# Reordering the first loads of a one-core kernel: w_in blocks paired with x tiles, the first block in column halves, the gate row from GpSimd, x tile 4 ahead of w_z1

## The chip, the core and the metric

The kernel runs on one core of one Trainium2 chip. Times are device microseconds of that core; a profiled execution also has a span, which runs from its first to its last instruction and is about 1.7 us shorter than the device time. The kernel before took 208.58 us (median of 3 runs, 208.38 to 208.61). The runs below were made on several chips, and each is compared with runs of the kernel before on its own chip.

## The reference, cut to what matters

```python
def _B_ref(x, w_in, w_sp, b_sp, w_out):
    z = _gelu(jnp.einsum('bsd,df->bsf', x, w_in))     # x 2048 x 512, w_in 512 x 1376
    z1 = z[..., :Fh].copy()                           # Fh = 688
    z2 = _layernorm(z[..., Fh:], axis=-1)
    g = jnp.einsum('ts,bsf->btf', w_sp, z2) + b_sp[None, :, None]
    return jnp.einsum('bsf,fd->bsd', z1 * g, w_out)
g = _sigmoid((x * gate_w).sum(-1, keepdims=True))
a = _A_ref(x, A_wqkv, A_w_phi, A_wo)                  # linear attention, not touched here
return g * a + (1 - g) * _B_ref(...)
```

The kernel starts with z2, the second half of the product of x and w_in. It contracts over 512, so it needs four blocks of 128 rows of w_in (blocks 0 to 3). The gate's logit rides along: the gate row is placed as column 689 beside the second half of each block.

## The kernel before: the parts that matter

The kernel works on 16 tiles of 128 rows of x. x tiles 0 to 3 are loaded plainly and transposed on TensorE; later tiles come through transposing loads. "Half 0" and "half 1" of a block are its columns 0 to 343 and 344 to 687; half 1 also has the gate's column, so its products need the gate row.

```python
    def load_z2w(eng, dt):                      # one block: 128 rows of 688 bf16, 172 KB
        eng.dma_start(out=w_z2[:, dt, 0:FH], in_=w_in_v[:, dt, FH:F])

    nc.sync.dma_start(out=xs[:, 0, :], in_=x2[0:P, :])
    load_z2w(nc.scalar, 0)
    nc.sync.dma_start(out=xs[:, 1, :], in_=x2[P:2 * P, :])
    load_z2w(nc.scalar, 1)
    load_z2w(nc.sync, 2)
    nc.scalar.dma_start(out=gaterow[0:NDT, :], in_=gate_w.rearrange("(dt p) -> dt p", p=P))
    load_z2w(nc.scalar, 3)
    nc.sync.dma_start(out=xs[:, 2:4, :], in_=...)            # x tiles 2 and 3, 256 KB
    for h in range(2):
        nc.sync.dma_start(out=w_z1[:, 2 * h:2 * h + 2, :], in_=...)
    for i in range(4, 8):
        nc.sync.dma_start_transpose(out=xT[:, :, i * P:(i + 1) * P], in_=...)
    ...
    # z2_first_two: one(tt, dt, j) is the product of x tile tt with half j of block dt
        warm_up(6)                  # 512-column products on constants
        warm_up(5, P)               # 128-column ones
        x_T(0, 0, 1, ...)           # TensorE transposes of x tile 0
        x_T(0, 1, NDT, ..., on_act=True)
        warm_up(3, P)
        one(0, 0, 0)
        x_T(1, 0, 2, ...)
        x_T(1, 2, NDT, ..., on_act=True)
        one(0, 1, 0)
        warm_up(2, P)
        one(1, 0, 0)
        one(1, 1, 0)
        gate_T()                    # gate row -> gate column of w_z2
        one(0, 2, 0)
        one(1, 2, 0)
        for dt in range(2):
            one(0, dt, 1)
            one(1, dt, 1)
        one(0, 2, 1)
        one(1, 2, 1)
        x_T(2, 0, NDT, ...)
        one(0, 3, 0); one(0, 3, 1); z2_out(0, zps[0])
        one(1, 3, 0); one(1, 3, 1); z2_out(1, zps[1])
        x_T(3, 0, NDT, ...)
    # then tiles 2, 3, ... in a steady stream of products
```

The softmax here doesn't subtract the row's maximum and nothing guards it: scores larger than these inputs give would overflow.

## Time and profile before

| kernel before, profiled run | us | view |
|---|---|---|
| span | 206.5 | page |
| TensorE busy | 201.1 (97%) | busy table |
| first transposes of x tile 0 | 3.70 | timeline |
| block 2 of w_in landed | 6.23 | chain of waits |
| last startup transposes end, steady stream begins | 8.63 | chain of waits |

The busy table of the kernel before (us, share of the span, instructions; PE is TensorE, DVE VectorE, ACT ScalarE, POOL GpSimd):

```profile
PE 201.1 (97%) x1530; PEld 120.3 (58%) x1548; DVE 129.1 (63%) x277; ACT 77.0 (37%) x124; POOL 44.6 (22%) x72
```

The waits of TensorE over the whole run. Columns: who waited, for whom, us in total, times, longest:

```profile
PE zp L215 <- PEq L582: 0.8, 1, 0.8
PE zp L184 <- DMA w_z<-in_B_w_in_dram: 0.7, 1, 0.7
```

The first 10 us of the chain of waits. Columns: start, duration, what; "x" counts merged instructions:

```profile
...
1.73 4.50 DMA w_z<-in_B_w_in_dram
...
6.27 1.33 PE zp L184 x8
7.60 0.22 PE pq L273 x4
7.83 0.58 PE zp L184 x4
8.41 0.22 PE pq L273 x4
8.63 1.46 PE zp L184 x10
```

TensorE is full except at the start, where it waits once, for block 2 (issued 1.73, landed 6.23). After it come 12 products (L184) and 8 transposes (L273), then the steady stream at 8.63. I call 8.63 the end of the startup in what follows; the prediction used 8.47, the start in the timeline of the first matmul after the transposes, whose modelled spans overlap. The change can act only on this startup.

### The profile page before, as it was taken

The page shows a single profiled execution, that of the slowest core. Times are in us where ns is not written, and L with a number is a line of the kernel's source. Part 1 is how long each engine was busy: PE and PEld are TensorE (multiplying, and loading weights), DVE is VectorE, ACT ScalarE, POOL GpSimd, SP SyncE. Part 2 cuts the span into 40 slices and gives each one's busy share as a digit, 9 for nine tenths or more (in the row PEclk, how much of TensorE's full clock was granted, in tenths as well). Part 3 has the DMA queues.
Part 4 walks back from the last instruction along what each step waited for, and adds up shares of the span by engine and source line. Part 5 has one row for each costly group of instructions (what it writes and reads, how often), then busy time and mean ns, then how long its engine had stood idle before and what let it go on. Part 6 is the DMA issues. An engine that isn't in the chain of part 4 may idle for free.

```text
span 206.5 us, 3955 instructions
## 1 busy us (share of the span) xinstructions
PE 201.1 (97%) x1530; PEld 120.3 (58%) x1548; DVE 129.1 (63%) x277; ACT 77.0 (37%) x124; POOL 44.6 (22%) x72
## 2 busy tenths in 40 slices
PE   8899999999999999999999999999999999999994
PEld 4666666655566555556565666555455555665543
DVE  3477665656977778879797788555466553633330
ACT  3666677786322243333424032222251126001322
POOL 3020202020532326244242422222204220200000
PEclk9999999999999999999999999999999999999999
DMA  6999399999996026961413218765565667453442
GB/s 184 274 149 210 79 263 211 251 206 259 193 290 136 3 38 127 309 100 22 91 29 63 51 38 116 141 117 68 106 158 39 130 104 190 53 104 75 120 97 81
DMA packets 89147, 27.22 MB, mean 132 GB/s; under 512 B 83144, under 2 KB 89128, under 8 KB 89128
## 3 DMA queue, kind: packets, MB, share of 16 engines
q1 hardware_dynamic: 86384, 24.37, 62.4%
q10 hardware_dynamic: 2744, 2.60, 3.8%
q8 instruction: 12, 0.20, 0.4%
q14 instruction: 7, 0.06, 0.1%
HBM read 4.41 MB, written 2.10 MB: 32 GB/s over the span
## 4 chain that ended last, share of the span: by engine, by line
PE 95%; DMA 2%; issue 1%; ACT 1%; SPq 0%; DVE 0%
PE mm L442 36%; PE zp L184 17%; PE mm L347 13%; PE mm L481 8%; PE mm L387 7%; PE mm L479 7%; DMA w_z<-in_B_w_in_dram 2%; PE at L455 2%; PE kvacc L403 2%; PE mm L484 1%; PE zp L300 0%; ACT z1all L253 0%; ACT wq_p L307 0%; PE pq L273 0%; SPq L120 0%
## 5 line engine op out<-in xcount | busy, mean ns | idle before, releaser
L442 PE MATMUL mm<-z2all,wspT 128*128 128x344 bf16 x512 | 79.9, 309 | 0.0
L442 PEld LDWEIGHTS <-wspT 128*128 128x128 bf16 x512 | 49.0, 98 | 25.7 <-issue 0.4
L184 PE MATMUL zp<-w_z,xT 128*128 128x344 bf16 (+1 forms) x256 | 38.8, 309 | 0.7 <-DMA w_z<-in_B_w_in_dram 0.7
L351 ACT ACTIVATE eq<-mm 128x512 bf16<-128x512 f32 x32 | 17.4, 594 | 51.3 <-PE mm L347 25.6
L355 DVE TENSOR_REDUCE zs<-eq 128x64 f32<-128x1024 bf16 x16 | 19.5, 1220 | 20.4 <-ACT eq L351 20.4
L184 PEld LDWEIGHTS <-xT 128*128 128x128 bf16 x256 | 24.6, 98 | 12.8 <-issue 0.7
L447 DVE SCALAR_TENSOR_TENSOR ucat<-mm,bT,z1all 128x344 bf16<-128x344 f32 x32 | 17.4, 544 | 21.9 <-PE mm L442 21.9
L364 POOL TENSOR_TENSOR eq<-eq,ratio 128x512 bf16<-128x512 bf16 x16 | 16.9, 1059 | 49.9 <-DVE ratio L363 41.7
L351 ACT ACTIVATE ek<-mm 128x512 bf16<-128x512 f32 x32 | 17.3, 600 | 27.4 <-PE mm L347 27.4
L495 ACT ACTIVATE ob<-mm,g_inv 128x512 bf16<-128x512 f32 (+1 forms) x16 | 10.9, 681 | 32.8 <-PE mm L484 28.0
L355 DVE TENSOR_REDUCE zs<-ek 128x64 f32<-128x1024 bf16 x16 | 19.3, 1209 | 2.8 <-ACT ek L351 2.8
L481 PE MATMUL mm<-wspT,uT 128*128 128x512 bf16 (+2 forms) x85 | 20.1, 366 | 0.0
L347 PEld LDWEIGHTS <-xT 128*128 128x128 bf16 x128 | 12.2, 98 | 13.2 <-PE mm L484 0.8
L364 POOL TENSOR_TENSOR ek<-ek,ratio 128x512 bf16<-128x512 bf16 x16 | 16.9, 1059 | 2.6 <-DVE ratio L363 1.6
L387 PE MATMUL mm<-wv_sb,xT 128*128 128x512 bf16 x64 | 16.4, 379 | 0.0
L347 PE MATMUL mm<-wq_p,xT 128*128 128x512 bf16 x55 | 16.0, 379 | 0.5
L347 PE MATMUL mm<-wk_p,xT 128*128 128x512 bf16 x61 | 16.1, 379 | 0.3
L479 PE MATMUL mm<-wspT,oT 128*128 128x512 bf16 (+2 forms) x62 | 15.6, 365 | 0.3
L202 DVE BATCH_NORM_STATS2 bn<-z2all 128x6 f32<-128x344 bf16 x32 | 14.9, 501 | 0.0
L199 ACT ACTIVATE z2all<-zp 128x688 bf16<-128x688 f32 x16 | 11.8, 744 | 7.0 <-PE zp L184 7.0
L253 ACT ACTIVATE z1all<-zp 128x688 bf16<-128x688 f32 x16 | 11.9, 744 | 5.1 <-PE zp L184 4.6
L481 PEld LDWEIGHTS <-uT 128*128 128x128 bf16 x85 | 8.1, 98 | 9.2
(71 smaller groups left out, 143.1 us busy)
## 6 DMA issues: line engine op xcount, KB each, us to landing
out_dram<-ob ACTq DMA_DIRECT2D x15, 128.0 KB, 2.0
wspT<-in_B_w_out_dram SPq DMA_DIRECT2D x2, 640.0 KB, 5.2
w_z<-in_B_w_in_dram SPq DMA_DIRECT2D x2, 344.0 KB, 4.7
w_z<-in_B_w_in_dram ACTq DMA_DIRECT2D x3, 172.0 KB, 3.4
wv_sb<-in_A_wqkv_dram SPq DMA_DIRECT2D x2, 256.0 KB, 2.9
wspT<-in_A_wo_dram SPq DMA_DIRECT2D x2, 256.0 KB, 3.9
xs<-in_A_x_dram SPq DMA_DIRECT2D x2, 128.0 KB, 3.0
xs<-in_A_x_dram SPq DMA_DIRECT2D x1, 256.0 KB, 5.1
```

Of the source, the lines that this page charges most:

```text
L184: nc.tensor.matmul(zp[:, j, 0:n], lhsT=xT[:, dt, tt * P:(tt + 1) * P], rhs=wt[:, dt, j * HF:j * HF + n], start=(dt == 0), stop=(dt == NDT ...
L202: nc.vector.bn_stats(out=bn6[:, tt, j, :], in_=z2v[:, j, :])
L253: nc.scalar.activation(out=z1all[:, tt, :].rearrange("p (j n) -> p j n", j=2), in_=zp[:, :, 0:HF], func=AF.Gelu_apprx_tanh,)
L347: nc.tensor.matmul(ps[:, :], lhsT=xT[:, dt, tt * P:(tt + 1) * P], rhs=w[:, dt, :], start=(dt == 0), stop=(dt == NDT - 1))
L351: nc.scalar.activation(out=e[:, :, a, :], in_=ps[:, :].rearrange("p (h f) -> p h f", f=DH), func=AF.Exp, scale=1.0 - 2.0 * a)
L355: nc.vector.tensor_reduce(out=z[:].rearrange("p h a -> p (h a)"), in_=e[:].rearrange("p h a f -> p (h a) f"), axis=AX.X, op=ALU.add,)
L364: nc.gpsimd.tensor_tensor(out=e[:, :, 1, :], in0=e[:, :, 1, :], in1=ratio[:, :, None].to_broadcast([P, H, DH]), op=ALU.mult)
L387: nc.tensor.matmul(v_ps[:, :], lhsT=xT[:, dt, tt * P:(tt + 1) * P], rhs=wv_sb[:, dt, :], start=(dt == 0), stop=(dt == NDT - 1))
L442: nc.tensor.matmul(gp[:, 0:HF], lhsT=wspT[:, st, tt * P:(tt + 1) * P], rhs=z2all[:, st, j * HF:(j + 1) * HF], start=(st == 0), stop=(st == ...
L447: nc.vector.scalar_tensor_tensor(out=ucat[tt % NU][:, c0 + j * HF:c0 + (j + 1) * HF], in0=gp[:, 0:HF], scalar=bT[:, tt:tt + 1], in1=z1all[ ...
L479: nc.tensor.matmul(acc, lhsT=oT[:, g, :], rhs=wo_t[:, g, c0:c1], start=(g == 0), stop=False)
L481: nc.tensor.matmul(acc, lhsT=uT[:, i + ft, :], rhs=w_main[i][:, ft, c0:c1], start=False, stop=False)
```

## The change

The intent: let each block of w_in flow beside an x tile, with a smaller first block, so that TensorE begins earlier and waits less; take the gate row's issue away from the ACT queue; fetch x tile 4 earlier. Fewer warm-up products fit in front of an earlier start. The diff, cut to its core (the new `first` argument of z_one, which lets half 1 start its sum with block 1, is left out):

```diff
+    nc.gpsimd.dma_start(out=gaterow[0:NDT, :], in_=gate_w.rearrange("(dt p) -> dt p", p=P))
     nc.sync.dma_start(out=xs[:, 0, :], in_=x2[0:P, :])
-    load_z2w(nc.scalar, 0)
+    nc.scalar.dma_start(out=w_z2[:, 0, 0:HF], in_=w_in_v[:, 0, FH:FH + HF])
     nc.sync.dma_start(out=xs[:, 1, :], in_=x2[P:2 * P, :])
     load_z2w(nc.scalar, 1)
-    load_z2w(nc.sync, 2)
-    nc.scalar.dma_start(out=gaterow[0:NDT, :], in_=gate_w.rearrange("(dt p) -> dt p", p=P))
-    load_z2w(nc.scalar, 3)
     nc.sync.dma_start(out=xs[:, 2:4, :], in_=...)
+    load_z2w(nc.scalar, 2)
+    nc.sync.dma_start(out=w_z2[:, 0, HF:FH], in_=w_in_v[:, 0, FH + HF:F])
+    load_z2w(nc.scalar, 3)
+    x_dma_T(4)                       # the transposing load of x tile 4
     for h in range(2):               # w_z1
...
-        warm_up(5, P)
+        warm_up(2, P)
-        x_T(0, 1, NDT, ..., on_act=True)
+        x_T(0, 1, NDT, ...)
-        warm_up(2, P)
+        warm_up(1, P)
...
-        for dt in range(2):
+        for dt in range(1, 3):       # half 1 of block 0 moves behind block 3
             one(0, dt, 1)
             one(1, dt, 1)
-        one(0, 2, 1); one(1, 2, 1)
         x_T(2, 0, NDT, ...)
-        one(0, 3, 0); one(0, 3, 1); z2_out(0, zps[0])
-        one(1, 3, 0); one(1, 3, 1); z2_out(1, zps[1])
+        for tt in range(2):
+            one(tt, 3, 0); one(tt, 0, 1); one(tt, 3, 1); z2_out(tt, zps[tt])
```

More of the change, by code (lines that the diff above doesn't have):

```diff
@@ L118, with x_dma_T @@
     nc.sync.dma_start(out=xs[:, 0, :], in_=x2[0:P, :])
-    load_z2w(nc.scalar, 0)
+    nc.scalar.dma_start(out=w_z2[:, 0, 0:HF], in_=w_in_v[:, 0, FH:FH + HF])
     nc.sync.dma_start(out=xs[:, 1, :], in_=x2[P:2 * P, :])
     load_z2w(nc.scalar, 1)
-    load_z2w(nc.sync, 2)
-    nc.scalar.dma_start(out=gaterow[0:NDT, :], in_=gate_w.rearrange("(dt p) -> dt p", p=P))
-    load_z2w(nc.scalar, 3)
     nc.sync.dma_start(
         out=xs[:, 2:4, :], in_=x2[2 * P:4 * P, :].rearrange("(i p) d -> p i d", p=P))
+    load_z2w(nc.scalar, 2)
+    nc.sync.dma_start(out=w_z2[:, 0, HF:FH], in_=w_in_v[:, 0, FH + HF:F])
+    load_z2w(nc.scalar, 3)
+    def x_dma_T(i):
+        nc.sync.dma_start_transpose(out=xT[:, :, i * P:(i + 1) * P], in_=x2[i * P:(i + 1) * P, :])
+    x_dma_T(4)
     for h in range(2):
@@ L129 @@
             out=w_z1[:, 2 * h:2 * h + 2, :], in_=w_in_v[:, 2 * h:2 * h + 2, 0:FH])
-    for i in range(4, 8):
-        nc.sync.dma_start_transpose(out=xT[:, :, i * P:(i + 1) * P], in_=x2[i * P:(i + 1) * P, :])
+    for i in range(5, 8):
+        x_dma_T(i)
     for q in range(2, NCH):
@@ L180, in pq_tile, with z_one @@
         return psF.tile(shape, dtype, name="pq", tag=next_turn("pq", 2))
-    def z_one(zp, tt, wt, w, dt, j):
+    def z_one(zp, tt, wt, w, dt, j, first=0):
         n = HF if j == 0 else w - HF
@@ L186, in z_one @@
             rhs=wt[:, dt, j * HF:j * HF + n],
-            start=(dt == 0), stop=(dt == NDT - 1),
+            start=(dt == first), stop=(dt == NDT - 1),
         )
@@ L219, in one @@
         def one(tt, dt, j):
-            z_one(zps[tt], tt, w_z2, FH + 1, dt, j)
+            z_one(zps[tt], tt, w_z2, FH + 1, dt, j, first=j)
         warm_up(6)
-        warm_up(5, P)
+        warm_up(2, P)
         x_T(0, 0, 1, pq_tile([P, 1, P], BF16)[:, :, :])
-        x_T(0, 1, NDT, pq_tile([P, 3, P], BF16)[:, :, :], on_act=True)
+        x_T(0, 1, NDT, pq_tile([P, 3, P], BF16)[:, :, :])
         warm_up(3, P)
@@ L236, in z2_first_two @@
         one(1, 2, 0)
-        for dt in range(2):
+        for dt in range(1, 3):
             one(0, dt, 1)
             one(1, dt, 1)
-        one(0, 2, 1)
-        one(1, 2, 1)
         x_T(2, 0, NDT, pq_tile([P, NDT, P], BF16)[:, :, :])
-        one(0, 3, 0)
-        one(0, 3, 1)
-        z2_out(0, zps[0])
-        one(1, 3, 0)
-        one(1, 3, 1)
-        z2_out(1, zps[1])
+        for tt in range(2):
+            one(tt, 3, 0)
+            one(tt, 0, 1)
+            one(tt, 3, 1)
+            z2_out(tt, zps[tt])
         x_T(3, 0, NDT, pq_tile([P, NDT, P], BF16)[:, :, :])
```

## The prediction

> **What bounds the kernel.** TensorE: busy 201.1 of 206.5 us (97%, busy table), 95% of the chain of waits. By the waits view it waits twice: 0.84 us before its first instruction and 0.66 us for a block of w_in. After the last startup transposes at 8.25 us (timeline) it lists no wait, so what the start gains or loses should pass to the end unshortened.
>
> **The start before.** Real work: 16 products (0.147 us apart) and 16 transposes (0.055 us apart): 3.2 us. It begins at 3.70 us, when x tile 0 has landed (issue 0.80 + 2.8), and ends at 8.47: about 1.6 us is lost to loads. Landings (DMA issues view): w_in block 0 3.8, x tile 1 4.5, block 1 4.6, block 2 6.2 (issued 1.73 + 4.5), block 3 6.9, x tiles 2-3 7.3. The chain's only DMA piece is block 2, 1.73 to 6.23. After it 12 products and 8 transposes run almost without a gap, 6.27 to 8.47: 12 x 0.147 + 8 x 0.055 = 2.2 us.
>
> The loads are 1.2 MB. From 2 to 8 us the DMA moves 260 to 357 GB/s (windows): bandwidth and order, not issue. The Trainium skill, "DMA: Bandwidth & Descriptors", section "Issuing engines are not separate DMA queues", says all issuers share the same 16 engines; pairing orders the bytes, it adds no rate.
>
> **The change.**
> - Block 0's first half is 86 KB less ahead of the first products: at 300 GB/s at most 0.3 us (estimate); it and x tile 0 land near 3.4. Three 128-column warm-ups go (0.2 us).
> - Block 2 goes third on the ACT queue, beside x tiles 2-3. About 86 KB fewer are ahead of it: landing 5.6 to 5.9. x tiles 2-3, now third on SP, about 6.3.
> - The first tiles' second-half products of block 0 move behind block 3. After block 2 there are still 12 products and 8 transposes, 2.2 us. But the second half of block 0 and block 3 are now the last bytes, landing 6.7 to 7.2; six products and four transposes (1.1 us) come after them. Startup ends 7.9 to 8.3 (before 8.47): gain 0.2 to 0.6.
> - The gate row on GpSimd frees 0.57 us of ACT issue. Same page, "Specifications": about 1 us to first byte on that path against 0.6. Issued near 1.5, landing estimated by 4.5; PE asks near 5.0.
> - x tile 0's three-block copy moves ACT to DVE: about 0.36 us against 0.48: neutral, block 1 arrives later anyway.
> - x tile 4's transposed load goes ahead of w_z1: 1.26 us of SP issue and 128 KB. w_z1 landed 8.2 and 9.1; now about 9 and 9.8, needed at 10.5 and 11.0. Slack shrinks from 2 to about 1 us.
>
> **Prediction.** 208.2 us, range 207.75 to 208.6. Faster by over 2% 0.01, within 2% 0.98, slower 0.01: the whole loss available is 1.6 us, under 1%.
>
> **What would show it.** The wait for block 2 ends before 6.0 (timeline); a wait appears on block 0's second half, block 3 or x tiles 2-3 near 6.7 to 7.1; the last startup transposes start 0.2 to 0.6 earlier; the first z1 product has no DMA wait; everything later shifts by that amount, durations equal.
>
> **What would make it wrong.** The gate row landing after block 2; w_z1 landing after 10.5, which gives the gain back; landings that follow slow DMA engines rather than bytes, so nothing lands earlier; the clock warming later with fewer warm-ups.

## The result and the profile after

The changed kernel took 208.32 us (median of 4 runs, 208.07 to 208.91); the kernel before 208.60 us (208.38 to 208.63) in runs that include those of the first section. The ratio is 0.9993, with a 95% interval of 0.9969 to 1.0017: the same.

The same three views of the changed kernel, whose profiled run took 208.54 us. The busy table:

```profile
PE 201.7 (98%) x1526; PEld 120.9 (58%) x1544; DVE 129.5 (63%) x278; ACT 76.5 (37%) x123; POOL 45.4 (22%) x73
```

The waits of TensorE, and from the chain of waits the pieces that answer to those of before:

```profile
PE zp L221 <- PEq L585: 0.8, 1, 0.8
PE zp L190 <- DMA w_z<-in_B_w_in_dram: 0.3, 1, 0.3
```

```profile
...
1.74 4.74 DMA w_z<-in_B_w_in_dram
...
6.52 1.04 PE zp L190 x6
7.56 0.22 PE pq L276 x4
7.78 0.88 PE zp L190 x6
...
8.89 16.35 PE zp L190 x112
```

The wait for block 2 is shorter (0.3 against 0.7 us) only because TensorE came to it later. Block 2 landed at 6.48, later than the 6.23 of before, and the startup ended at 8.89, 0.26 us later. Two lines of the timeline show why TensorE was late as well. Columns: start, us, engine, line, operation, shapes:

```profile
...
4.32 0.49 PE L190 MATMUL zp<-w_z,xT 128*128 128x344 bf16 x1
...
6.52 1.04 PE L190 MATMUL zp<-w_z,xT 128*128 128x344 bf16 x6 [0.32 <-DMA w_z<-in_B_w_in_dram]
```

A product that takes 0.49 us is one at half clock; with the full clock it takes 0.31. The trace's clock record gives the full clock from 6.06 us on in this run, from 3.47 in the profiled run of before. TensorE was also held by its own warm-up products: x tile 0 had landed at 3.29 us, and its first transpose started at 3.57.

A trace also records, for every load, when each of the 16 DMA engines reported its share. The Trainium skill ("DMA: Bandwidth & Descriptors", section "Why a DMA increments its semaphore by 16 and not by 1") says that only the full count of 16 means that all data has landed. The traces agree: TensorE went on within 0.05 us of the last report. So a load is as late as its slowest engine. I use this for block 2 below: "median" is the middle of its 16 reports, "last" its landing.

### The profile page after: what moved, and what is told of

The parts are those of the page before. It is cut to its first block, busy times and chain, and to the rows that moved or that the text cites. A ratio compares the mean times of both kernels' runs of the same rounds, so it can differ in the third digit from the quotient of the medians.

```text
span 206.8 us, 3948 instructions
## 1 busy us (share of the span) xinstructions
PE 201.7 (98%) x1526; PEld 120.9 (58%) x1544; DVE 129.5 (63%) x278; ACT 76.5 (37%) x123; POOL 45.4 (22%) x73
## 4 chain that ended last, share of the span: by engine, by line
PE 94%; DMA 2%; ACT 1%; issue 1%; ACTq 0%; DVE 0%
PE mm L445 36%; PE zp L190 17%; PE mm L350 13%; PE mm L484 8%; PE mm L390 7%; PE mm L482 7%; DMA w_z<-in_B_w_in_dram 2%; PE at L458 2%; PE kvacc L406 2%; PE mm L487 1%; PE zp L303 0%; ACT z1all L256 0%; ACT wq_p L310 0%; ACTq L117 0%; PE pq L276 0%
## 5 line engine op out<-in xcount | busy, mean ns | idle before, releaser
L190 PE MATMUL zp<-w_z,xT 128*128 128x344 bf16 (+1 forms) x256 | 39.3, 312 | 0.3 <-DMA w_z<-in_B_w_in_dram 0.3
```

What stands on the lines that cost most here:

```text
L190: nc.tensor.matmul(zp[:, j, 0:n], lhsT=xT[:, dt, tt * P:(tt + 1) * P], rhs=wt[:, dt, j * HF:j * HF + n], start=(dt == first), stop=(dt == ...
```

## The experiments

All 12 runs gave the right result. The edits are against the changed kernel unless another is named.

### One law behind them all

The end of the startup and the span, read from the chain of waits of the profiled runs:

| profiled run | startup ends | span | difference |
|---|---|---|---|
| before | 8.63 | 206.48 | 197.85 |
| changed kernel | 8.89 | 206.83 | 197.94 |
| rep_after | 8.45 | 206.36 | 197.91 |
| xT4_back2 | 11.13 | 209.05 | 197.92 |
| warm_back | 9.46 | 207.38 | 197.92 |
| w2_sp | 10.07 | 207.99 | 197.92 |
| before_fewwarm | 8.04 | 205.92 | 197.88 |
| after_whole | 8.46 | 206.44 | 197.98 |

The end of the startup moves over 3.1 us, the rest stays within 0.13 us. (The profiles that the table leaves out, xT4_back, gate_act, xT4_fill, before_gpgate and v1, have 197.92 to 198.02.) Next to nothing is won or lost after the startup in these runs; each experiment can be read from its first 11 us. (v2 is an exception: 9.30 and 207.75, with a later wait of 0.3 us for an attention transpose.)

### rep_after: the changed kernel again

> The changed kernel once more, for its spread and a second profile. Clock theory: its four runs of 208.07 to 208.91 us differ because TensorE gets its full clock at a different moment each time (6.06 us after the start in the profiled run of 208.54, 3.47 us in the profiled run of before), so a run with an early clock shows products 0.147 us apart from the start and a span near 206.4, one with a late clock a span near 206.8 to 207.2. Loads theory: the clock does not matter, since TensorE waits for block 2 of w_in anyway (0.32 us at 6.52); the spread then goes with the landing of block 2 (6.5 in the profile) and of what follows it.

Measured: 208.59 us (208.08 to 208.75), before on the same chip 208.10 (207.75 to 208.25); ratio 1.0020 (1.0007 to 1.0032). So on this chip the changed kernel is slower, by a fifth of a per cent. The profiled run was its fastest:

```profile
...
1.75 4.30 DMA w_z<-in_B_w_in_dram
...
6.09 1.04 PE zp L190 x6
```

The clock came at 5.47 us, in the other profile at 6.06: both before block 2's landing, so the clock cost little there. The startup's end moved with block 2: landed 6.05 and 6.48, ended 8.45 and 8.89. That speaks for the loads theory.

### xT4_back and xT4_back2: x tile 4 behind w_z1 again

```diff
-    x_dma_T(4)
     for h in range(2):   # w_z1
...
-    for i in range(5, 8):
+    for i in range(4, 8):
         x_dma_T(i)
```

> The changed kernel with x tile 4's transposed load back behind w_z1. Loads theory: that load's 256-byte packets (first at 5.54 us) sit among the last packets of block 3, of block 0's second half and of x tiles 2-3, some of which took 0.6 to 1.0 us there; without it these land about 0.4 us earlier (block 3 near 7.0 instead of 7.4), the last startup transposes start 0.2 to 0.4 us earlier and the median falls to 207.9 to 208.1. Rival: the load is harmless, the slow packets come from the bandwidth limit; the median stays within 0.1 us of the changed kernel's of the same rounds.

Measured: 209.18 us (208.38 to 209.62), ratio 1.0057 (1.0045 to 1.0069). The guess that the early transposing load disturbs was wrong in sign: without it the kernel is slower, by about 0.6 us of median on the same chip. Its half about the landings came true in the profile: block 3 landed at 6.83 us and the second half of block 0 at 6.51, against 7.02 and 6.80 in rep_after. But block 2, TensorE's last wait, did not land earlier (6.33 against 6.05). Its profiled run was again the fastest one.

> The kernel of xT4_back once more, for a second profile: its profiled run was its fastest (208.38 us, block 2 landed 6.33, startup ended 8.73) and does not show why its other runs took 208.9 to 209.6. Tail theory: in a slow run block 2 of w_in, or what comes after it, lands on one or two of the 16 DMA engines 0.5 to 1 us after the others (7.0 or later), and the span is 197.9 us plus the end of the startup. Clock theory: block 2 lands near 6.3 again, but TensorE runs at half clock until 7 us or later, products 0.29 us apart after block 2.

Measured: 209.43 us (208.40 to 210.90), ratio 1.0069 (1.0032 to 1.0106), profiled run 210.77. Its waits, its chain, and the windows view of the two windows that the clock record marks (columns: stretch, its length, busy us of each engine, granted clock, DMA share, GB/s):

```profile
PE pq L285 <- DMA gaterow<-in_gate_w_dram: 0.9, 1, 0.9
PE zp L220 <- PEq L584: 0.8, 1, 0.8
PE zp L189 <- DMA w_z<-in_B_w_in_dram: 0.5, 1, 0.5
```

```profile
...
1.75 5.31 DMA w_z<-in_B_w_in_dram
...
7.09 1.78 PE zp L189 x6
8.88 0.43 PE pq L275 x4
9.30 1.60 PE zp L189 x6
10.90 0.22 PE pq L275 x4
11.13 16.35 PE zp L189 x112
```

```profile
3.82:7.23 3.41, 1.94 (x18) 1.01 (x17) 1.02 (x4) 1.85 (x3) 0.00 (x0) 1.00 0.96 289
7.23:10.64 3.41, 3.41 (x16) 2.03 (x15) 0.42 (x1) 0.43 (x1) 0.00 (x0) 0.50 1.34 244
```

Both theories hold in this run, in sequence. Block 2's median engine reported at 5.66, its last three at 6.84, 7.03 and 7.05. With the gate row late too, TensorE was busy only 1.94 us of the window 3.82 to 7.23, and in the next window the granted clock was 0.50: the same six products took 1.78 us, against 1.04 in rep_after. The Trainium skill ("TensorE: Matmul & The Clock Gate", section "What's actually happening") describes a free-running window of 3413 ns; how busy TensorE was in it decides the clock. The records agree on its length: this clock changed at 3.82, 7.23 and 10.64.

The list of runs agrees: the two slowest of the six, 210.77 and 210.90 us, had a granted clock of 0.991, the other four, 208.40 to 209.76, had 0.998 or more. A late load can thus cost twice, once as a wait and once as a half clock after it; but the first xT4_back had a clock of 1.0 in all its runs and was slow all the same. Why the transposing load of x tile 4 helps when it stands ahead of w_z1 is not settled: the profiles of the two orders have block 2's last report at 6.05, 6.48 and at 6.33, 7.05, which overlap.

### warm_back: the old warm-ups

```diff
-        warm_up(2, P)
+        warm_up(5, P)
...
-        warm_up(1, P)
+        warm_up(2, P)
```

> The changed kernel with the warm-up products of before (5 and 2 small ones instead of 2 and 1). Clock theory: the late clock of the changed kernel comes from the fewer warm-ups; with them back the full clock comes near 3.5 us as before and the spread of the runs shrinks to 0.25 us, median 208.0 to 208.2. Rival: the moment of the clock is set by something outside the kernel; the spread and the median stay those of the changed kernel, within 0.1 us.

Measured: 208.84 us (208.53 to 209.25), ratio 1.0039 (1.0026 to 1.0051). The clock came at 4.00 us in this profile, and yet the run took 209.09 us: the gate row landed late (TensorE waited 0.66 us for it) and block 2 at 6.95. More warm-ups neither narrowed the runs nor helped; the clock theory, as an explanation of the changed kernel's spread, falls here. Whether fewer warm-ups delay the full clock stays open: it came between 3.82 and 6.46 us in the nine profiles with fewer that have a clock record, between 3.47 and 4.47 in the three with the old number. What the trace does show is their direct cost in this order of loads: x tile 0 landed at 3.24 us, but its first transpose started only at 3.89, behind the five small warm-ups, against 3.57 behind two in rep_after (landed 3.27).

### gate_act: the gate row back on ACT

```diff
-    nc.gpsimd.dma_start(out=gaterow[0:NDT, :], ...)
...
     load_z2w(nc.scalar, 1)
+    nc.scalar.dma_start(out=gaterow[0:NDT, :], ...)
```

> The changed kernel with the gate row's load back on the ACT queue, third there, so that blocks 2 and 3 are issued 0.6 us later. If the GpSimd issue is a gain, the median rises by 0.1 to 0.4 us, block 2 landing near 6.8. If block 2 is limited by bandwidth and not by its issue (issued 1.74, landed 6.5), nothing moves: within 0.1 us, block 2 at 6.4 to 6.6. If the gate row on GpSimd costs something (it landed 5.6), the median falls.

Measured: 208.25 us (207.94 to 209.23), ratio 1.0015 (0.9998 to 1.0033), not to be told from rep_after. (Its median is 0.34 us below rep_after's, but the intervals overlap, so the time does not decide between the three expectations.) Block 2 was issued 0.6 us later, at 2.35, and landed at 6.47, as expected where the issue is not the limit. The run has a side effect that I had not foreseen: it makes nine loads on the two hardware queues instead of eight. The ninth waited for the first to land and held up the ACT engine, whose first table load then began at 3.92 us instead of 2.73. This is a use of the GpSimd issue that the intent did not name: it keeps the count at eight.

### before_gpgate: one part of the change alone

The kernel before, with the gate row from GpSimd and nothing else:

```diff
+    nc.gpsimd.dma_start(out=gaterow[0:NDT, :], ...)
     nc.gpsimd.memset(brow[:], 0.0)
...
-    nc.scalar.dma_start(out=gaterow[0:NDT, :], ...)
```

> The kernel before with one part of the change: the gate row's load from GpSimd. Theory: in the kernel before, the gate row on the ACT queue leaves that queue almost empty from 4.0 to 4.5 us (12 KB), so block 2 on the SP queue has the DMA engines to itself and lands on its median engine at 4.94 us, against 5.3 to 5.5 in the changed kernels. With the gate row away from ACT, block 3 runs beside block 2: block 2's median landing 5.2 to 5.4, its last 6.3 to 6.9, time 0.1 to 0.6 us longer than before. Rival (the intent of the change): the ACT queue gets free 0.57 us earlier, block 3 lands earlier and the time is equal or up to 0.2 us shorter.

Measured: 208.30 us (208.14 to 208.42), ratio 1.0006 (0.9993 to 1.0019). Block 2's median report was 5.12, its last 5.37, so the theory's 6.3 to 6.9 is refuted. The gate row on GpSimd by itself does nothing to the time that these runs can tell.

### before_fewwarm: another part alone

The kernel before with `warm_up(2, P)` for `warm_up(5, P)` and `warm_up(1, P)` for `warm_up(2, P)`, four small products fewer.

> The kernel before with the changed kernel's fewer warm-up products (2 and 1 small ones for 5 and 2), loads and order as before. Clock theory: fewer warm-ups delay the full clock (5.5 to 6.1 us in four profiles with fewer, 3.5 and 4.0 in two with more), so the median rises by 0.2 to 0.5 us and the runs spread over more than 0.5 us. Rival: TensorE waits for block 2 until 6.2 anyway, so the warm-ups do not matter: the median within 0.1 us of before, the spread under 0.5 us.

Measured: 207.68 us (207.55 to 208.43), before on the same chip 208.14 (207.74 to 208.50); ratio 0.9983 (0.9967 to 0.9998). Both theories missed, the clock theory in sign. The chain of its profiled run, which has no wait for a load after x tile 0:

```profile
...
0.80 2.99 DMA xs<-in_A_x_dram
...
3.83 0.40 PE pq L273 x4
4.23 0.17 PE zp L215 x3
...
5.67 1.34 PE zp L184 x8
7.01 0.22 PE pq L273 x4
7.23 0.58 PE zp L184 x4
7.82 0.22 PE pq L273 x4
8.04 16.35 PE zp L184 x112
```

Block 2 landed at 5.22 here, not at 6.23 as in the first profile of the same loads. So TensorE itself is the limit from x tile 0 on in this profile. Why fewer warm-ups help is shown only in part, though. Three of the four dropped ones stood before the landing of x tile 0, so they cost only what outlasts it. v1 has the old warm-ups and the same loads, on the same chip, and in its timeline the first transposes start at the same moment:

```profile
...
3.83 0.38 PE L272 MATMUL pq<-ident,xs 128*128 128x128 bf16 x4
```

From the landing of x tile 0 to this start it took 0.05 us here (3.79 to 3.83), 0.12 in v1 (3.71 to 3.83) and 0.19 in before_gpgate, with the old warm-ups and at half clock there (3.70 to 3.89). So the three cost some 0.07 to 0.15 us, and the fourth 0.06 at full clock. That is 0.13 to 0.2 us of the 0.46 by which the median fell; the rest is open, and the interval of the ratio reaches up to 0.9998.

### v1: products moved into the wait

The kernel before, with the four half-1 products of blocks 0 and 1 ahead of block 2's, and x tile 2's transposes after tile 0's last products.

> The kernel before, loads untouched, with TensorE's startup in another order: the four second-half products of blocks 0 and 1 before the products of block 2 (they fill its wait), and x tile 2's transposes after tile 0's last products. If the startup ends when the last landing has been used up, and not with the number of bytes, then the products fill the 0.66 us wait: the wait for block 2 falls to 0 to 0.1 us, the startup ends 8.1 to 8.2 instead of 8.47, and the time falls by 0.3 to 0.5 us. If it falls by less than 0.1 us, the last landings (x tiles 2-3 at 7.35, block 3 at 6.84) are what holds the end of the startup.

Measured: 208.43 us (208.09 to 209.04), ratio 1.0015 (0.9998 to 1.0032): a miss. In its profile block 2 landed at 5.26, so there was no wait to fill, and the moved products waited 0.30 us for the gate's column. I had designed it for the wait of one profile.

### w2_sp: block 2 back on the SP queue

```diff
+    load_z2w(nc.sync, 2)           # third on SP, before x tiles 2-3
...
-    load_z2w(nc.scalar, 2)
-    nc.sync.dma_start(out=w_z2[:, 0, HF:FH], ...)
+    nc.scalar.dma_start(out=w_z2[:, 0, HF:FH], ...)
```

> The changed kernel with block 2 of w_in third on the SP queue, before x tiles 2-3, as it was before the change; the second half of block 0 takes its place on the ACT queue. Queue theory: in the changed order block 2 shares the DMA with 256 KB of x tiles 2-3 and lands on its median engine at 5.3 to 5.7 us, its last engine at 6.05 to 7.05; ahead of x tiles 2-3 its median falls to 4.9 to 5.2 and its last to 5.3 to 5.9, the wait for it shrinks below 0.1 us or becomes the gate row's, and the median time falls by 0.2 to 0.5 us against the changed kernel (208.59 on its chip, 1.002 of before), to about 0.999 of before. Tail theory: the last engine lags whatever the order, block 2's last landing stays at 6.0 to 7.0, and the ratio to before stays at 1.001 to 1.003.

Measured: 208.84 us (208.27 to 209.71), ratio 1.0040 (1.0022 to 1.0059), the profiled run the slowest. Block 2's median report came at 5.58, the 14th at 5.72, the last at 7.41, and TensorE waited for it:

```profile
PE zp L190 <- DMA w_z<-in_B_w_in_dram: 1.2, 1, 1.2
```

The last load in its chain is another one, x tiles 2-3, which landed at 8.53 us, just as the six products after block 2 were through:

```profile
...
2.25 6.28 DMA xs<-in_A_x_dram
...
8.57 0.40 PE pq L276 x4
```

Block 2 was late in this order too, with two engines of 16 over a microsecond behind the others; so its place beside x tiles 2-3 is not needed for the lag.

### xT4_fill: the waits filled

The kernel of xT4_back with `warm_up(4, P)` before `gate_T()` and `warm_up(8, P)` after it.

> The kernel of xT4_back with twelve small products that keep TensorE busy where it waits for the gate row and block 2 (four before the gate row's transpose, eight after). Clock theory: its slow runs (209.0 to 210.9 us) come from the clock falling back to half after a window with about 1.4 us of waiting (7.23 to 10.64 us in the second profile); with the waits partly filled the runs above 209.4 disappear and the median falls from 209.2 to 209.4 to 208.4 to 208.9, though the filling itself costs up to 0.3 us where block 2 is on time. Tail theory alone: the runs stay spread to 209.6 and above, median within 0.2 us.

Measured: 209.08 us (208.42 to 209.70), ratio 1.0049 (1.0030 to 1.0068). The clock stayed full from 4.60 us on in its profile and no run was above 209.70, where xT4_back2 had two near 210.8; but two of six were above 209.4 and the median is 0.2 us above the expected band. All its runs had a clock of 1.0, but so had those of the first xT4_back without filling. So the half clock can explain the two slowest runs of xT4_back2 (one was profiled) and no more; the rest is as the tail theory alone had it. In the profile the loads are late: the gate row landed at 6.52, block 2 at 6.72. (The two kernels ran on different chips.)

### v2: a try at a faster version

The kernel of before_fewwarm with block 0 in halves, the second half third on ACT, and one 512-column warm-up less.

> A try for a version faster than both: the kernel before with fewer warm-ups (before_fewwarm, 207.68 us) and block 0 in column halves, the second half third on the ACT queue, one 512-column warm-up less. x tile 0 lands near 3.3 us (3.26 to 3.29 in all profiles with the half block, 3.6 to 3.8 without), so TensorE can start 0.3 us earlier. If the startup is limited by TensorE from there on: 207.3 to 207.6 us. If block 1 at 4.6 or block 2 at 5.2 is the limit: equal to before_fewwarm, 0.998 of before.

Measured: 209.56 us (209.03 to 210.65), ratio 1.0076 (1.0055 to 1.0096): a clear miss. It repeats the mistake of gate_act with nine loads. Block 3 could be issued only at 3.48 us, the ACT engine's table load moved to 3.87, and TensorE waited for x tile 0's copy on ACT:

```profile
PE zp L185 <- ACT xT L277: 1.1, 1, 1.1
```

So the time of this run says nothing about the half block. Its profile does: with the loads of before_fewwarm but for the halves and the later gate row and block 3, block 2's last report came 1.1 us after its median (table below), against 0.11 in before_fewwarm. (x tile 0 lands with the half block at 3.24 to 3.35 us in the profiles made before v2, a little wider than I had written.)

### after_whole: block 0 whole again

```diff
-    nc.scalar.dma_start(out=w_z2[:, 0, 0:HF], in_=w_in_v[:, 0, FH:FH + HF])
+    load_z2w(nc.scalar, 0)
...
-    nc.sync.dma_start(out=w_z2[:, 0, HF:FH], in_=w_in_v[:, 0, FH + HF:F])
+    nc.sync.dma_start(out=brow[0:NT, :], ...)   # 4 KB, keeps the number of loads
```

> The changed kernel with block 0 of w_in whole again (one load, first on the ACT queue); the small load of the spatial bias takes the place of its second half, so that the count of loads and all later waits stay. Half-block theory: one to three of the 16 DMA engines lag 0.5 to 1.9 us in every profile with the 688-byte rows of the half blocks (block 2: 14th landing 5.5 to 6.8, last 6.05 to 7.2), and not in before_fewwarm and v1 (block 2: all within 5.26), so with 1376-byte rows alone block 2 lands by 5.6, the runs lie within 0.5 us and the ratio to before falls from 1.002 to 0.998 to 1.000. Rival: the lag belongs to the other parts (x tiles 2-3 beside block 2, x tile 4's transposed load, the gate row on GpSimd): last landing of block 2 again 6.0 to 7.0, ratio 1.001 to 1.004, runs spread over 0.7 us or more.

Measured: 208.45 us (208.15 to 208.60), ratio 1.0019 (1.0006 to 1.0032). The lag is gone as the half-block theory had it: block 2's median report 5.91, its last 6.01, and the runs spread over 0.45 us. But block 2 did not land by 5.6, and the time did not fall; both that theory had wrong. Its chain shows the new limit, with no load in it:

```profile
...
0.84 2.93 PE zp L220 x8
...
3.81 0.61 PE pq L275 x4
4.41 0.32 PE zp L220 x3
...
6.09 1.04 PE zp L189 x6
7.13 0.22 PE pq L275 x4
7.36 0.88 PE zp L189 x6
8.24 0.22 PE pq L275 x4
8.46 16.35 PE zp L189 x112
```

x tile 0 now lands at 3.76 us instead of 3.27 in rep_after; TensorE's first transposes start at 3.81 instead of 3.57, it works at half clock until 5.28 and reaches block 2 only when that has landed. The DMA rates from 3 to 5 us (windows view, last column) of rep_after, then of after_whole (w2_sp, on the same chip as after_whole, had 311 and 214):

```profile
3.00:4.00 1.00, 1.00 (x8) 0.72 (x7) 0.08 (x1) 1.00 (x1) 0.37 (x2) 1.00 1.03 318
4.00:5.00 1.00, 1.00 (x10) 0.86 (x9) 0.50 (x2) 0.02 (x1) 0.00 (x0) 1.00 0.97 300
```

```profile
3.00:4.00 1.00, 0.97 (x7) 0.42 (x6) 0.00 (x0) 1.00 (x1) 0.36 (x2) 1.00 1.10 392
4.00:5.00 1.00, 1.00 (x10) 0.86 (x9) 0.58 (x2) 0.01 (x1) 0.00 (x0) 1.00 1.08 373
```

Block 2 in all profiles, with the sums moved before 3 us and from 3 to 5 us:

| profiled run | block 0 | median | 14th | last | KB before 3 us | KB, 3 to 5 us |
|---|---|---|---|---|---|---|
| before | whole | 4.94 | 5.78 | 6.23 | 285 | 615 |
| before_gpgate (chip 4) | whole | 5.12 | 5.22 | 5.37 | 219 | 746 |
| before_fewwarm (chip 4) | whole | 5.11 | 5.17 | 5.22 | 217 | 739 |
| v1 (chip 4) | whole | 5.12 | 5.21 | 5.26 | 192 | 738 |
| after_whole (chip 2) | whole | 5.91 | 5.98 | 6.01 | 191 | 765 |
| changed kernel | halves | 5.46 | 5.88 | 6.48 | 286 | 592 |
| rep_after (chip 13) | halves | 5.45 | 5.89 | 6.05 | 290 | 618 |
| xT4_back (chip 13) | halves | 5.31 | 5.54 | 6.33 | 287 | 635 |
| warm_back (chip 13) | halves | 5.48 | 6.11 | 6.95 | 301 | 565 |
| gate_act (chip 13) | halves | 5.82 | 6.27 | 6.47 | 254 | 653 |
| xT4_back2 (chip 4) | halves | 5.66 | 6.84 | 7.05 | 284 | 520 |
| w2_sp (chip 2) | halves | 5.58 | 5.72 | 7.41 | 245 | 525 |
| xT4_fill (chip 2) | halves | 5.39 | 6.58 | 6.72 | 247 | 563 |
| v2 (chip 2) | halves | 4.86 | 5.12 | 5.97 | 268 | 624 |

(The chips are numbered as the results list them; for the first two profiles none is listed.) With halves the last engine is 0.6 to 1.8 us behind the median in all nine profiles; with a whole block 0.1 to 0.25 us in four of five. The exception is the very first profile of the kernel before, the one that the prediction was built on. So the lag goes with the half block in every profile, and something else can bring it too (in before_gpgate one engine was 1 us late for x tiles 2-3). Only the swap in after_whole isolates the half block, with one profile, and it changes the row length and the order of the bytes at once.

That short rows are the cause is not shown, and the packets in the trace speak against it. The median packet of 688 bytes took 34 ns, that of 1376 bytes 59 ns. In rep_after no packet of 688 bytes started from 3 to 4 us, and 17 of them from 4 to 5; the rate was low all the same, because single packets of other loads took up to 0.6 us. Another split fits all 14 profiles, the exception too: without the lag 191 to 219 KB had moved before 3 us, with it 245 to 301. So the lag goes with an early flow of data, and the low sum from 3 to 5 us partly makes up for more before it. This split was found after the runs; none of them tests it, and why engines fall behind stays open.

## Why the prediction was right, and where its reasoning was not

The number was right: 208.2 us predicted, 208.32 measured, within the stated range of 207.75 to 208.6. In part that was luck. That the change could move little (at most 1.6 us) was reasoned, and right; but the interval of the ratio includes no gain at all, the forecast gain did not show on another chip (1.0020), the startup ended later in the profiled run, and some steps failed.

- **"What the start gains or loses should pass to the end unshortened": right.** The rest of the span stayed at 197.85 to 198.02 us in all profiles but v2's while the startup's end moved from 8.04 to 11.13.
- **First half of block 0 and x tile 0 "land near 3.4": right.** 3.45 and 3.29, against 3.76 and 3.58 in the profile of before. But TensorE used little of it: its warm-ups held it until 3.57 (3.70 before).
- **"Block 2 ... landing 5.6 to 5.9": wrong, and this is the step that failed.** I counted bytes ahead of it. That gives about the median engine (5.46). The landing is the last engine's report, 6.48, and between 5.97 and 7.41 in the half-block profiles. I had named the case ("landings that follow slow DMA engines rather than bytes") but gave it no weight in the sum. The wait that I expected on the last bytes, near 6.7 to 7.1, does not appear; block 2 is again the only load that TensorE waits for.
- **x tiles 2-3 "about 6.3", block 3 and the second half "6.7 to 7.2": too early.** x tiles 2-3 landed at 6.94 by their last engine (median 5.71), so for the same reason. Block 3 landed at 7.44 and the second half at 7.50; block 3's median was already at 7.34, so there it is not only the last engine.
- **"Startup ends 7.9 to 8.3 (before 8.47)": wrong in the profiled run.** On the prediction's measure it was 8.72, later than before. In rep_after, where block 2 landed at 6.05, it was 8.29.
- **"About 1.6 us is lost to loads": true of that one execution only.** In before_fewwarm, with the same loads, TensorE waited for none after x tile 0. One profile of a startup does not tell its usual limit.
- **Gate row "landing estimated by 4.5": mis-sized by over 1 us.** It landed at 5.66; its last engine was late as well (median 4.48). In the changed kernel it still came before block 2; in xT4_back2 it cost 0.9 us.
- **w_z1 "now about 9 and 9.8", with no DMA wait: right.** 8.90 and 9.98, and no wait for it is listed.
- **Fewer warm-ups: counted as making room (0.2 us), and feared for the clock.** Alone they are the best part of the change, 0.9983 on the kernel before (0.9967 to 0.9998), for a reason that the profiles show only in part.

Put together, the parts seem to work against each other. The half block starts TensorE about 0.25 us earlier (3.57 against 3.81 us in after_whole) and comes with late last engines; the kernel before with fewer warm-ups had a median 0.46 us lower; the gate row moves nothing by itself; x tile 4 ahead of w_z1 is needed in this order (1.0057 without it, against 1.0020). The sum was measured, and is about zero; that it is made up of these terms is argued, not shown. The version with the best ratio here is before_fewwarm: the old loads with the fewer warm-ups, 207.68 us, 0.17% faster than before on its chip.

## What to carry to other kernels

A load is as late as the slowest of its 16 DMA engines: compare the median and the last report before counting bytes, and do not plan a startup from a single profile. A wait early in a kernel may be paid twice, once as idle time and once as half clock in the window after it; on the other hand, warm-up products that outlast the first landing hold up the real work: x tile 0 landed near 3.25 us, and its transposes began at 3.57 us behind two small warm-ups (rep_after), at 3.89 behind five (warm_back). Keep the number of loads in flight in mind when adding one, for it may wait for the first to land.

## What the Trainium skill lacked or had wrong

- "TensorE: Matmul & The Clock Gate", section "What's actually happening", has the clock fall back after an idle window. Here it fell to 0.50 after a window in which TensorE was busy 1.94 of 3.41 us (xT4_back2). Windows with 2.17 us busy (v2, 3.97 to 7.38) and 2.35 (warm_back, 4.00 to 7.41) kept it. The busy times are modelled; the page gives no share that counts as idle.
- "DMA: Bandwidth & Descriptors", "Specifications", gives 512 bytes as the size from which transfers run at line rate. Here the median packet of 688 bytes took 34 ns (20 bytes per ns), that of 1024 bytes 46 (22) and that of 1376 bytes 59 (23), so the rate still rose by some 15% above 688 bytes.
- The same page, "Latency and other measured facts", calls engines 7 and 15 usually slower and ties that, as a best guess, to loads issued from GpSimd. Here one or two of 16 engines lagged also without any such load: block 2's 14th report 5.12, its last 5.97 in v2; 5.78 and 6.23 in the kernel before. The reports do not say which engines these were.
- The same page, "Specifications", has about 1 us to the first byte on the GpSimd path. The gate row of 1 KB, issued at 1.42 us, had its first packet 2.2 to 3.1 us later and took 3.5 to 5.1 us to land beside busy queues (nine profiles); no page gives a landing time for a small load under such traffic.
- No page says how many loads may be in flight before the next waits. Here the ninth on the two hardware queues waited for the first to land (landed 3.46 us, ninth issued 3.48 in v2); this may be the doing of the programming layer and not of the chip.
